# Sparse attention and a GELU layer on one core: the order of the first loads, and of two tables of work, is changed

## The chip, the core and the metric

The kernel runs on one core of a Trainium2 chip. A core has five engines, each with its own instruction stream: TensorE (PE in the profile, with its weight loads as PEld), VectorE (DVE), ScalarE (ACT), GpSimd (POOL) and SyncE (SP). They meet through semaphores. Transfers are asked for by POOL (software queue) or SP (hardware queue) and moved by 16 DMA engines that all of them share. The metric is the device time of one execution in microseconds (us); lower is better.

## The reference

Block-sparse attention over 4 batches, 8 heads, 768 positions, head size 64, in blocks of 32 (24 blocks). Its output, laid out by token, goes through a two-layer network with an exact GELU.

```python
scores = scale * np.matmul(q, k.transpose(0, 1, 3, 2))
mask = np.abs(blk_i - blk_j) <= window                      # window 1
mask = mask | (blk_i == 0) | (blk_j == 0) | (blk_i == n_blocks - 1) | (blk_j == n_blocks - 1)
for qb in range(n_blocks):
    for kb in sampled_blocks[qb]:                           # 3 drawn blocks
        mask[qb * block:(qb + 1) * block, kb * block:(kb + 1) * block] = True
scores = np.where(mask, scores, -1000000000.0)
attn = exp(scores - max) / (sum + 1e-09)
x = (attn @ v) laid out as [3072 tokens, 512]
h = x @ w_in                                                # 512 x 2048
out = (0.5 * h * (1.0 + erf(h / sqrt(2)))) @ w_out          # 2048 x 512
```

## The kernel before

The work is cut into eight units, two to a batch, of three blocks of 128 tokens each. A unit has an attention stage, then the first layer (`ffn1_step`, L551: w_in against the unit's `xT`, GELU into `g`); its second layer (`ffn2_pieces`, L576: `g` against w_out) is spread as filler over the attention stage of the next unit. The first unit of a batch also does the two dense rows of blocks (rounds 0 to 3); the other rounds take two query blocks each and form groups (`groups`; for the first unit group 0, 1 and 2).

What stands in which order is written out by hand. `attention` (L616) reads a string of words for each unit: `s` scores on PE, `m` maxima on DVE, `e` exponentials on ACT, `t` turning on DVE, `w` values on PE, `d` division on DVE, `o`/`O` outputs (PE, then ACT), `f3` three products of filler on PE, `S` the store of a finished block, `G` the load of the GELU table, `x...` a named extra step. The first unit's string stands at L731 and its filler is idle products that feed nothing (L589); the second's is `PLANS[1]` (L749), where `xk0` to `xk3` and `xq0` to `xq3` turn a pair of heads of the second batch's k or q on PE (L242) and place it by ACT, or by DVE with a `d` behind.

The first unit is fed by POOL, and POOL's order is the program's order of the calls from L181 on: k and q of batch 0, eight requests for V (`load_values`, one per head, L149), the numbers of the sampled blocks (`block_numbers`, L231, a load into the engine's registers, per group), then copies of the sampled key blocks (`gather`, L317, out of `k0`, which lies in the tile qT), then by `values_of` (L706) copies of the sampled value blocks out of `kv` into free places in `kn` (group 0) and `g` (groups 1, 2). Between these stand the requests for w_in in quarters (`load_w_in`, L162) and for w_out in halves (`load_w_out`, L167); behind the last copy, by `later_keys` (L719), those for k and q of batch 1, in halves of four heads.

SP carries six small transfers out of `k0` into `gb` early on (`fixed(t, nc.sync, 1)`, L303 to L307: the first and last key block for groups 1 and 2, 96 KB each), and all stores. The software requests take eight semaphores in turn, so each waits for the landing of the eighth before it.

Of the kernel before, what the change touches and what calls it, by code (L numbers as in the profile page):

```python
# [11 lines left out]
BF16 = mybir.dt.bfloat16  # L12
# [8 lines left out]
def kernel(  # L21
# [10 lines left out]
    nc = tc.nc  # L32
    P = 128
    B, H, S, D = q.shape
# [9 lines left out]
    VS = 2 * D + 4  # L44
    KC = NPR * BL
# [13 lines left out]
    const = ctx.enter_context(tc.tile_pool(name="const", bufs=1))  # L59
# [11 lines left out]
    kvs = [const.tile([P, NB + 1, BW], BF16, name=f"kv{i}") for i in range(2)]  # L71
# [10 lines left out]
    g = const.tile([P, KOUT, UT], BF16, name="g")  # L82
    mark = const.tile([1, 1], BF16, name="mark")
    junk = const.tile([1, 1], BF16, name="junk")

    HALVES = (slice(0, 4), slice(4, 8))

# [57 lines left out]
    def load_v(b, h):  # L145
        G, hh = divmod(h, 4)
        c0 = KC + VS * G + D * (hh % 2)
        hh ^= G
        nc.gpsimd.dma_start(out=kvs[b % 2][32 * hh:32 * hh + 32, 0:NB, c0:c0 + D],  # L149
                            in_=v[b, h].rearrange("(n p) d -> p n d", p=BL))  # L150


    VORDER = sorted(range(H), key=lambda h: (h // 4, (h % 4 ^ h // 4) % 2, h % 4))

    def load_values(b, at=slice(None)):
        for h in VORDER[at]:
            load_v(b, h)

    def load_w_in(part, n=4):
        w = D_FF // n  # L160
        cols = slice(w * part, w * part + w)
        nc.gpsimd.dma_start(  # L162
            out=w_in_sb[:, :, cols], in_=moe_w_in[:, cols].rearrange("(ki p) f -> p ki f", p=P))

    def load_w_out(part, n=4):
        w = KOUT // n
        nc.gpsimd.dma_start(  # L167
            out=w_out_sb[:, w * part:w * part + w, :],
            in_=moe_w_out[P * w * part:P * w * (part + 1)].rearrange("(ko p) f -> p ko f", p=P))
# [5 lines left out]
    def ones(i):  # L175
        for hh in range(4):
            for G in range(2):
# [6 lines left out]
                      in_=bass.AP(tensor=sb_words, offset=0,  # L184
                                  ap=[[NB * NR * 2, 1], [1, NB * NR * 2]]))
# [40 lines left out]
    def block_numbers(js, engine):  # L226
        flat = vf.rearrange("o j r -> o (j r)")
        vals = []
        for c0 in range(js[0] * NR, (js[-1] + 1) * NR, 22):
            c1 = min(c0 + 22, (js[-1] + 1) * NR)  # L230
            _, got = nc.values_load_multi_w_load_instructions(  # L231
                flat[0:1, c0:c1], engines=[engine], min_val=0, max_val=NB,
                skip_runtime_bounds_check_because="block numbers are below the number of blocks")
            vals += got if isinstance(got, (tuple, list)) else [got]
        return {j: vals[NR * i:NR * i + NR] for i, j in enumerate(js)}
# [46 lines left out]
    def gather_fixed(kT, place, copy=None, part=None, lanes=range(3)):  # L282

        copy = copy or nc.vector.tensor_copy
        groups = gb.rearrange("p (g x) -> p g x", x=GW)
        js = sorted(place)
        runs = [[j for j in js if place[j] - j == c] for c in sorted({place[j] - j for j in js})]
        for run in runs if part != 1 else ():
            i0 = place[run[0]]
            assert i0 % 3 == 0  # L290
            for lane in range(min(3, len(run))):
                if lane not in lanes:
                    continue
                m, g0 = len(range(lane, len(run), 3)), i0 // 3
                c0, j = BW + KC * lane, run[0] + lane - 1
                copy(
                    groups[:, g0:g0 + m, c0:c0 + 3 * BW].rearrange("p g (w c) -> p g w c", c=BW)[:, :, :, 0:KC],
                    kT[:, j:j + 3 * m, :].rearrange("p (g w) c -> p g w c", w=3))
        if part == 0:
            return  # L300
        at = slice(min(place.values()) // 3, max(place.values()) // 3 + 1)
        n = at.stop - at.start
        for to, n0 in ((groups[:, at, 0:3 * KC].rearrange("p g (l c) -> p g l c", c=KC), 0),  # L303
                       (groups[:, at, 4 * BW:GW].rearrange("p g (l x) -> p g l x", x=DW)[:, :, :, NR * BW:DW], NB - 1)):
            if copy is nc.sync:
                for x in range(n):
                    nc.sync.dma_start(out=to[:, x], in_=kT[:, n0:n0 + 1, :].to_broadcast([P, 3, KC]))  # L307
            else:
                copy(to, kT[:, None, n0:n0 + 1, :].to_broadcast([P, n, 3, KC]))

    def gather(unit, js, at, c0=0, c1=BW, engine=None):

        src = k0 if (unit.b, c1) == (0, KC) else kvs[unit.b % 2][:, :, c0:c1]
        for j in js:
            for r in range(NR):
                to = sampled_values(unit, j, r) if c0 == KC else sampled(unit.place[j], r)[:, c0:c1]
                (engine or nc.vector).tensor_copy(to[:, None, :], src[:, bass.ds(at[j][r], 1), :])  # L317
# [271 lines left out]
    def idle_products(m):  # L589

        op = psO.tile([P, D_MODEL], F32, name="op", tag="op")
        for _ in range(m):
            nc.tensor.matmul(op, lhsT=identity, rhs=qT0[:, 0:2, 0:2, :], start=True, stop=True)
            yield
# [77 lines left out]
    grps = units[0].groups  # L672
    value_list()
    others = block_numbers(grps[1], POOL)
    load_values(0, slice(3, 7))
    others |= block_numbers(grps[2], POOL)
    load_values(0, slice(7, None))
    known = block_numbers(grps[0], DVE)
    nc.vector.memset(kvs[1][:, FILLED:NB + 1, KC:BW], 0.0)
    known |= block_numbers(J0[7:9], DVE)  # L680
# [14 lines left out]
    def fixed(t, *how):  # L695
        gather_fixed(k0, {j: units[0].place[j] for j in grps[t]}, *how)
    fixed(1, nc.sync, 1)
    fixed(2, nc.sync, 1)
    gather(units[0], grps[1][:2], others, 0, KC, nc.gpsimd)
    load_w_in(0)  # L700
# [5 lines left out]
    def values_of(t):  # L706

        def ask():
            js = grps[t]
            gather(units[0], js[:3], others, KC, BW, nc.gpsimd)  # L710
            if t != 1:
                load_w_in(2 + t // 2)
            gather(units[0], js[3:], others, KC, BW, nc.gpsimd)
            if t == 2:
                load_w_out(0, 2)
                load_w_out(1, 2)
        return ask
# [7 lines left out]
    def more_numbers(js):  # L725
        def load():
            for c in range(0, len(js), 6):
                known.update(block_numbers(js[c:c + 6], DVE))
        return load
    attention(units[0], idle_products(32),  # L730
# [3 lines left out]
              {"l": later_keys, "p2": partial(later_pair, 0), "p3": partial(later_pair, 1),  # L734
               "h": lambda: fixed(0, None, 0, (0,)), "i": lambda: fixed(0, None, 0, (1, 2)),
               "j": lambda: fixed(0, None, 1),
# [7 lines left out]
    def next_keys(b):  # L744
# [1 line left out]
        spare_key(keys(b))  # L746

    PLANS = {
# [17 lines left out]
    for n, unit in enumerate(units):  # L766
# [3 lines left out]
        if nxt is not None and not fresh:  # L770
            if n == 0:
                nc.vector.tensor_copy(kvs[0][:, :, 0:KC], k0)
                more_numbers(J1[3:8])()
            gather_fixed(keys(b), nxt.place)
            gather(nxt, J1[:8], known)
            if n == 0:
                more_numbers(J0[:3])()
        for s in range(KOUT // 2):
            ffn1_step(n, 2 * s)
            if s == 0:  # L780
# [4 lines left out]
                elif fresh and b + 2 < B:  # L785
                    xT, t0 = column[b, unit.groups[-2][0]]
# [17 lines left out]
            if fresh and s == 0:  # L804
                gather_fixed(keys(b + 1), nxt.place)
                gather(nxt, J0[3:9], known)
                gather(nxt, J0[:3], known)
                hold_loads(sampled(nxt.place[J0[2]], NR - 1)[0:1, BW - 1:BW])
                gather(nxt, J0[9:], others, engine=nc.gpsimd)
# [43 lines left out]
```

## Time and profile before

| | |
|---|---|
| runs, median of 3 | 274.44 us (274.05 to 274.59) |
| profiled execution, device time | 273.89 us |
| its span, first to last instruction | 271.9 us |
| mean granted TensorE clock | 0.994 |
| busy: PE / DVE / ACT / POOL | 255.1 / 203.2 / 207.0 / 103.0 us |

The profile's times count from the span's first instruction. A row of the timeline gives start, length, engine, source line, operation, tiles written and read, count, and in brackets how long the engine had been idle and what ended that. A row of the stretches gives the busy time (and instruction count) of PE, PEld, DVE, ACT and POOL, the granted TensorE clock, the DMA engines' mean share and the GB/s moved. "issue" is a wait for nothing that the profile shows.

### The profile page before, as it was taken

What the parts mean: (1) busy time and instruction counts of PE and PEld (TensorE: products, weight loads), DVE (VectorE), ACT (ScalarE), POOL (GpSimd) and SP (SyncE); (2) the same over time, 40 slices, a digit from 0 to 9 for tenths busy, and PEclk for the clock granted to TensorE, in tenths of its full rate; (3) what the DMA queues carried; (4) which work ended last, traced back from release to release, by engine and by line L of the source; (5) the groups of instructions that cost most, each with busy time, mean ns of one, the idle gap of its engine ahead of it and who ended that gap; (6) DMA issues with size and microseconds to landing.
All of it is one profiled execution on the core that took longest, in us unless ns stands there. A gap on an engine that the chain in (4) does not pass through costs nothing.

```text
span 271.9 us, 11545 instructions
## 1 busy us (share of the span) xinstructions
PE 255.1 (94%) x4944; PEld 144.8 (53%) x4944; DVE 203.2 (75%) x472; ACT 207.0 (76%) x379; POOL 103.0 (38%) x212
## 2 busy tenths in 40 slices
PE   0789699999999999999999999999999999999995
PEld 0634485455664665545554466455645655465544
DVE  7599758699896989589998987698939993882000
ACT  8789746977868886797868976988788966995611
POOL 7798960735964000950963002920040160000000
PEclk9999979999999999999999999999999999999999
DMA  6999399979999115951999108911101110111012
GB/s 98 185 185 144 66 140 201 206 129 146 95 172 129 41 43 122 122 65 50 104 164 123 60 28 159 112 43 45 40 0 41 46 41 0 41 41 43 0 40 78
DMA packets 75909, 24.40 MB, mean 90 GB/s; under 512 B 65489, under 2 KB 72914, under 8 KB 75858
## 3 DMA queue, kind: packets, MB, share of 16 engines
q0 software_dynamic: 57440, 13.64, 53.7%
q1 hardware_dynamic: 18418, 10.03, 15.5%
q8 instruction: 38, 0.62, 1.0%
q14 instruction: 13, 0.11, 0.1%
HBM read 27.26 MB, written 6.29 MB: 123 GB/s over the span
## 4 chain that ended last, share of the span: by engine, by line
PE 71%; DMA 9%; ACT 7%; POOL 6%; issue 4%; DVE 2%; POOLq 1%; ACTq 0%
PE hp L540 27%; PE op L583 21%; PE av L484 9%; DMA kn<-in_k_dram 6%; PE sc L358 4%; DMA kv<-in_v_dram 3%; ACT L429 2%; PE tx L516 2%; PE op L612 2%; PE av L445 2%; POOL g L317 2%; ACT pp L401 2%; PE pt L242 1%; POOL kv L149 1%; PE av L612 1%
## 5 line engine op out<-in xcount | busy, mean ns | idle before, releaser
L540 PE MATMUL hp<-xT,w_in_sb 128*128 128x384 bf16 (+2 forms) x536 | 85.1, 319 | 0.2 <-issue 0.2
L583 PE MATMUL op<-w_out_sb,g 128*128 128x512 bf16 x336 | 83.9, 380 | 0.4 <-issue 0.4
L401 ACT ACTIVATE pp<-sc,nm 128x256 bf16<-128x256 f32 x176 | 74.4, 546 | 7.5 <-DVE nm L384 7.5
L540 PEld LDWEIGHTS <-w_in_sb 128*128 128x128 bf16 x536 | 51.2, 98 | 33.3 <-issue 0.3
L562 ACT ACTIVATE g<-hp 128x768 bf16<-128x768 f32 x56 | 45.2, 809 | 25.4 <-PE hp L540 25.4
L384 DVE TENSOR_REDUCE nm<-sc 128x4 f32<-128x1024 f32 (+1 forms) x48 | 53.2, 1117 | 10.5 <-PE sc L358 10.2
L583 PEld LDWEIGHTS <-g 128*128 128x128 bf16 x336 | 28.6, 98 | 34.3 <-issue 7.2
L317 DVE COPY gb<-kv 128x392 bf16 x177 | 34.7, 274 | 0.0
L418 DVE STREAM_TRANSPOSE pT<-pp 128x512 f32<-128x512 f32 (+1 forms) x48 | 31.2, 657 | 4.3 <-ACT pp L401 3.8
L317 POOL COPY gb<-kv 128x392 bf16 x54 | 26.3, 537 | 16.1 <-PE av L484 15.7
L173 POOL COPY mark<-gb 1x1 bf16<-1x1 bf16 x6 | 1.1, 178 | 81.3 <-DVE gb L317 81.3
L484 PE MATMUL av<-kv,pT 64*32 64x130 bf16 (+1 forms) x1344 | 28.7, 228 | 1.0 <-DVE pT L418 0.9
L484 PEld LDWEIGHTS <-pT 64*32 64x32 bf16 (+1 forms) x2400 | 26.8, 94 | 5.1 <-DVE pT L418 2.6
L149 POOL DMA_DIRECT2D kv<-in_v_dram x32 | 22.9, 726 | 2.4 <-issue 2.3
L524 ACT COPY xT<-tx 128x512 bf16<-128x512 bf16 (+1 forms) x32 | 13.9, 459 | 11.6 <-PE tx L516 11.3
L358 PE MATMUL sc<-gb,qT 64*32 64x256 bf16 x704 | 18.4, 274 | 2.9 <-issue 1.5
L358 PEld LDWEIGHTS <-qT 64*32 64x32 bf16 x832 | 9.5, 89 | 21.2 <-issue 13.4
L429 ACT ACT_TABLE_LOAD x15 | 19.2, 1283 | 0.2
L387 DVE TENSOR_REDUCE nm<-sc 128x1 f32<-128x768 f32 x16 | 14.7, 947 | 5.9 <-PE sc L358 5.7
L504 DVE TENSOR_TENSOR xh<-av,rec 128x512 bf16<-128x512 f32 (+2 forms) x28 | 18.3, 652 | 1.0
L567 ACT COPY os<-op 128x512 f32<-128x512 f32 (+1 forms) x23 | 13.1, 570 | 6.0 <-PE op L612 4.3
L484 PE MATMUL av<-gb,pT 64*32 64x130 bf16 x924 | 17.2, 222 | 0.0
(80 smaller groups left out, 249.6 us busy)
## 6 DMA issues: line engine op xcount, KB each, us to landing
out_dram<-os SPq DMA_DIRECT2D x23, 256.0 KB, 2.4
kv<-in_v_dram POOLq DMA_DIRECT2D x32, 96.0 KB, 3.7
w_in_sb<-in_moe_w_in_dram POOLq DMA_DIRECT2D x4, 512.0 KB, 7.3
w_out_sb<-in_moe_w_out_dram POOLq DMA_DIRECT2D x2, 1024.0 KB, 13.4
kn<-in_k_dram POOLq DMA_DIRECT2D x4, 384.0 KB, 11.4
qn<-in_q_dram POOLq DMA_DIRECT2D x4, 384.0 KB, 12.8
qn<-in_q_dram POOLq DMA_DIRECT2D x12, 128.0 KB, 4.9
kn<-in_k_dram POOLq DMA_DIRECT2D x12, 128.0 KB, 6.0
```

Source lines behind the costliest of these rows:

```text
L149: nc.gpsimd.dma_start(out=kvs[b % 2][32 * hh:32 * hh + 32, 0:NB, c0:c0 + D], in_=v[b, h].rearrange("(n p) d -> p n d", p=BL))
L317: (engine or nc.vector).tensor_copy(to[:, None, :], src[:, bass.ds(at[j][r], 1), :])
L358: nc.tensor.matmul(o, lhsT=qT[rows, j // 4, pr, BL * (j % 4):BL * (j % 4) + BL], rhs=rhs(rows, pr), start=True, stop=True)
L384: nc.vector.tensor_reduce(out=nm[:, 0:2 * n].rearrange("p (g j) -> p g j", g=2), in_=A4[:, :, 0:n, :], op=ALU.max, axis=AX.X, negate=True)
L401: nc.scalar.activation(at[:, x // n, x % n], A[:, a:a + 256].rearrange("p (e c k) -> p e c k", e=2, k=BL), AF.Exp, bias=nm[:, x:x + 1])
L418: nc.vector.transpose(pt.rearrange("p g c x -> p (g c) x")[:, :, 64 * s:64 * (s + n)].bitcast(F32), pp[:, 0:512 * n].bitcast(F32).rearrang ...
L429: nc.scalar.activation(junk, zero[0:1, 0:1], func)
L484: nc.tensor.matmul(av[32 * s:32 * (s + w), h, VS * G:VS * G + V2], lhsT=pv[rows, G, c % 4, BL * s:BL * (s + w), c // 4], rhs=src[rows], st ...
L504: nc.vector.tensor_tensor(xh[rows, :, 0:m * D].rearrange("p h (g x d) -> p h g x d", x=2, d=D), a[:, :, :, 0:2 * D].rearrange("p h g (x d) ...
L540: nc.tensor.matmul(hp[:, i, c0:c1], lhsT=w_in_sb[:, ki, (m + i) * P:(m + i + 1) * P], rhs=xTs[n % 2][:, ki, c0:c1], start=(ki == 0), stop= ...
L562: nc.scalar.activation(g[:, m:m + 2, 0:T], hp[:, :, 0:T], AF.Gelu)
L583: nc.tensor.matmul(op, lhsT=g[:, m, t * P:(t + 1) * P], rhs=w_out_sb[:, m, :], start=(m == 0), stop=(m == KOUT - 1))
```

## The change

It has four parts. POOL asks for the last V part ahead of loading group 2's numbers. SP gets a transfer of two values out of the last V part into a new tile `seen`, ahead of group 2's two key transfers: it waits for that part to land, and the two behind it with it. The third quarter of w_in, which stood among group 0's value copies, is asked for with the fourth, behind the last value copy. The strings of the first unit and of `PLANS[1]` are written anew. (`gather_fixed` names an expression; that changes nothing.)

```diff
+    seen = const.tile([1, 2], BF16, name="seen")
...
     others = block_numbers(grps[1], POOL)
-    load_values(0, slice(3, 7))
+    load_values(0, slice(3, None))
     others |= block_numbers(grps[2], POOL)
-    load_values(0, slice(7, None))
     known = block_numbers(grps[0], DVE)
...
     fixed(1, nc.sync, 1)
+
+    hh, c0 = VORDER[-1] % 4 ^ VORDER[-1] // 4, KC + VS * (VORDER[-1] // 4) + D * (VORDER[-1] % 2)
+    nc.sync.dma_start(out=seen, in_=kvs[0][32 * hh:32 * hh + 1, 0, c0:c0 + 2])
     fixed(2, nc.sync, 1)
...
             gather(units[0], js[:3], others, KC, BW, nc.gpsimd)
-            if t != 1:
-                load_w_in(2 + t // 2)
+            if t == 2:
+                load_w_in(2)
+                load_w_in(3)
             gather(units[0], js[3:], others, KC, BW, nc.gpsimd)
...
     PLANS = {
-        1: ("S s0 s1 m0 m1 f8 e0 f5 xk0d t0 f3 e1 s2 f3 xk1 m2 S t1 s3 e2 f3 m3 f2 xq1d xv t2 wa da e3  "
...
+        1: ("S s0 m0 s1 m1 e0 f10 e1 f3 t0 s2 xk1 t1 f3 m2 s3 f2 m3 xk0 f5 xq0d e2 f1 wa s4 e3 xk3 t2 da  "
...
```

Group 2 has three blocks, so `js[3:]` is empty there and both quarters stand behind the last value copy. On POOL, at the start, the V requests (`kv0`) and the loads of numbers (`vf`) stood like this, with what each waits for:

```order
L149 DMA kv0_86<-in_v_dram 32x24x64 x3
L231 TENSOR_LOAD vf_127 [waits DVE_49]
L149 DMA kv0_86<-in_v_dram 32x24x64
L149 DMA kv0_86<-in_v_dram 32x24x64 [waits DMASW0_49]
L149 DMA kv0_86<-in_v_dram 32x24x64 [waits DMASW1_49]
L149 DMA kv0_86<-in_v_dram 32x24x64 [waits DMASW2_49]
L231 TENSOR_LOAD vf_127
L149 DMA kv0_86<-in_v_dram 32x24x64 [waits DMASW3_49]
```

and now, at the same place:

```order
L150 DMA kv0_86<-in_v_dram 32x24x64 x3
L232 TENSOR_LOAD vf_128 [waits DVE_49]
L150 DMA kv0_86<-in_v_dram 32x24x64
L150 DMA kv0_86<-in_v_dram 32x24x64 [waits DMASW0_49]
L150 DMA kv0_86<-in_v_dram 32x24x64 [waits DMASW1_49]
L150 DMA kv0_86<-in_v_dram 32x24x64 [waits DMASW2_49]
L150 DMA kv0_86<-in_v_dram 32x24x64 [waits DMASW3_49]
L232 TENSOR_LOAD vf_128
```

The last request stands ahead of the second load of numbers. It still waits for DMASW3, the semaphore of q's second half. On POOL behind the value copies, where the weights and the next batch are asked for, the rows before were (the third quarter of w_in stands 49 rows ahead of the first of them, with group 0's copies):

```order
L162 DMA w_in_sb<-in_moe_w_in_dram 128x4x512
L167 DMA w_out_sb<-in_moe_w_out_dram 128x8x512 x2
L118 DMA kn<-in_k_dram 96x4x512
L118 DMA qn<-in_q_dram 96x4x512
L118 DMA kn<-in_k_dram 96x4x512
L118 DMA qn<-in_q_dram 96x4x512
```

and they now are:

```order
L163 DMA w_in_sb<-in_moe_w_in_dram 128x4x512 x2
L168 DMA w_out_sb<-in_moe_w_out_dram 128x8x512 x2
L119 DMA kn<-in_k_dram 96x4x512
L119 DMA qn<-in_q_dram 96x4x512
L119 DMA kn<-in_k_dram 96x4x512
L119 DMA qn<-in_q_dram 96x4x512
```

Two quarters of w_in now stand ahead of w_out and of the next batch's k and q. On PE, at the start of the second unit's attention stage, the first products of filler (`op`) and the first turn of the next batch's k (the weight load of `kn`) stood so, with the round of scores that comes next:

```order
L583 MATMUL op_1454<-w_out_sb_85,g_96 128x512 [waits DMASW0_49]
...
L583 MATMUL op_1454<-w_out_sb_85,g_96 128x512 [waits DMASW1_49]
...
L242 LDWEIGHTS kn_91 [waits DMASW2_49]
...
L583 LDWEIGHTS g_96 [waits Activation_49]
...
L358 LDWEIGHTS qT0_89 [waits DVE_49]
```

and now:

```order
L585 MATMUL op_1461<-w_out_sb_85,g_96 128x512 [waits DMASW0_49]
...
L585 MATMUL op_1461<-w_out_sb_85,g_96 128x512 [waits DMASW1_49]
...
L360 LDWEIGHTS qT0_89 [waits DVE_49]
L360 MATMUL sc_1482<-gb_88,qT0_89 32x256 [waits Activation_49]
...
L243 LDWEIGHTS kn_91 [waits DMASW2_49]
```

DMASW0 and DMASW1 are the two halves of w_out, read by the first and the ninth product; DMASW2 is the first half of k. The third round of scores has moved ahead of the first turn of k; the thirteen products and their two waits stand where they stood.

More of the change, by code (lines that the diff above doesn't have):

```diff
@@ L304, in gather_fixed @@
                        (groups[:, at, 4 * BW:GW].rearrange("p g (l x) -> p g l x", x=DW)[:, :, :, NR * BW:DW], NB - 1)):
+            fixed_block = kT[:, None, n0:n0 + 1, :].to_broadcast([P, n, 3, KC])
             if copy is nc.sync:
                 for x in range(n):
-                    nc.sync.dma_start(out=to[:, x], in_=kT[:, n0:n0 + 1, :].to_broadcast([P, 3, KC]))
+                    nc.sync.dma_start(out=to[:, x], in_=fixed_block[:, x])
             else:
-                copy(to, kT[:, None, n0:n0 + 1, :].to_broadcast([P, n, 3, KC]))
+                copy(to, fixed_block)
     def gather(unit, js, at, c0=0, c1=BW, engine=None):
```

10 rows, old and new, of tables (PLANS, js) are left out of this document.

## The prediction

> **What bounds the kernel now.** I read the page first, then the chain of work that ended last. TensorE (PE) is busy 94% of the span, so only PE's waits can be won. The chain over the first 76 us holds one long step that is not PE:
>
> ```profile
> PE 255.1 (94%) x4944; PEld 144.8 (53%) x4944; DVE 203.2 (75%) x472; ACT 207.0 (76%) x379; POOL 103.0 (38%) x212
> ```
> ```profile
> 33.55 0.69 POOL w_in_sb L162
> 34.24 1.73 POOL w_out_sb L167 x2
> 35.97 16.87 DMA kn<-in_k_dram
> 52.84 0.04 issue
> 52.88 0.53 PE pt L242 x16
> ...
> 66.92 0.44 issue
> ```
>
> GpSimd (POOL) asks for w_in's last quarter at 33.5, then for both halves of w_out, then for the second batch's k and q; PE's first turn of that k (the `pt` at 52.88) waits for it. Up to there the program runs at the pace of this row of transfers, which starts when POOL has made its last value copy. I then asked for POOL's timeline, the landings, and the stretches:
>
> ```profile
> 8.70 2.83 POOL L149 DMA_DIRECT2D kv<-in_v_dram  x4 [0.25 <-issue]
> 12.99 0.71 POOL L149 DMA_DIRECT2D kv<-in_v_dram  x1 [1.46 <-issue]
> 13.75 1.47 POOL L317 COPY gb<-qT 128x128 bf16 x6
> ...
> 18.24 2.17 POOL L317 COPY gb<-qT 128x128 bf16 x9
> 21.24 3.20 POOL L317 COPY kn<-kv 128x264 bf16 x9 [0.84 <-DMA kv<-in_v_dram]
> 24.39 0.74 POOL L162 DMA_DIRECT2D w_in_sb<-in_moe_w_in_dram  x1
> 25.12 1.10 POOL L317 COPY kn<-kv 128x264 bf16 x3
> 26.16 7.38 POOL L317 COPY g<-kv 128x264 bf16 x21
> 33.50 0.74 POOL L162 DMA_DIRECT2D w_in_sb<-in_moe_w_in_dram  x1
> 34.23 1.77 POOL L167 DMA_DIRECT2D w_out_sb<-in_moe_w_out_dram  x2
> ```
> ```profile
> DMA to landing us min/median/max: 10.9/13.4/15.9
> ```
> ```profile
> 30.00:32.00 2.00, 0.67 (x7) 0.31 (x6) 0.47 (x2) 0.91 (x3) 2.00 (x7) 1.00 0.00 0
> ...
> 34.00:36.00 2.00, 2.00 (x144) 2.00 (x132) 0.99 (x3) 0.00 (x0) 2.00 (x4) 0.50 0.47 22
> 36.00:38.00 2.00, 1.65 (x48) 1.28 (x31) 1.12 (x4) 0.58 (x1) 2.00 (x5) 0.81 1.19 196
> ...
> 50.00:52.00 2.00, 2.00 (x11) 0.88 (x9) 1.98 (x2) 1.99 (x5) 2.00 (x5) 1.00 1.24 206
> ```
>
> The last two figures of a stretch are DMA share and GB/s. The DMA is empty from 30 to about 35.5, then moves some 200 GB/s without a break. The landing row is that of w_out's two requests (34.23 and about 35.12): its second half lands 15.9 after 35.12, at 51.02. PE's own rows show how close that is:
>
> ```profile
> 27.08 0.41 PE L358 MATMUL sc<-gb,qT 64*32 64x256 bf16 x16 [0.35 <-ACT pp L401]
> ...
> 29.57 0.29 PE L358 MATMUL sc<-gb,qT 64*32 64x256 bf16 x4
> 31.33 0.29 PE L358 MATMUL sc<-gb,qT 64*32 64x256 bf16 x4 [1.47 <-issue]
> ...
> 49.44 2.98 PE L583 MATMUL op<-w_out_sb,g 128*128 128x512 bf16 x13
> 52.88 0.53 PE L242 MATMUL pt<-identity,kn 96*64 96x96 bf16 x16 [0.47 <-DMA kn<-in_k_dram]
> ```
> ```profile
> 258.10 3.45 PE op L612 x16
> ```
>
> Sixteen products of that size take 3.45 us, 0.216 each, so the ninth of those begun at 49.44, the first to read w_out's second half, stands at 51.17: 0.15 us after the landing. Then k's wait of 0.47. PE and the transfers are level here; whatever makes the transfers later is paid in full.
>
> **The change part by part.** *V ahead of the third group's numbers.* The last V request cannot leave before the second half of q has landed, since the software DMAs take eight semaphores in turn and it is the twelfth (the fourth was q's second half). PE saw that half at 12.02:
>
> ```profile
> 12.02 0.85 PE L242 MATMUL pt<-identity,qn 96*64 96x96 bf16 x16 [0.57 <-DMA qn<-in_q_dram]
> ```
>
> So it leaves at about 12.05 instead of 12.99. The numbers' load now stands behind it. Its 1.46 us either overlaps the request (copies from 13.5) or follows it (12.76 + 1.46 = 14.2), against 13.75 before: 0.25 earlier to 0.45 later. I take 0.2 later. The key copies then end at 20.41 + 0.2 = 20.6 (20.41 is the end of the row at 18.24). V's last part landed at 20.92:
>
> ```profile
> 12.99 7.93 DMA kv<-in_v_dram
> ```
>
> It gains at most the 0.94 of its earlier request, and is helped by the two of six key transfers (96 KB each, 0.2 MB, 1.0 us at 200 GB/s) that SyncE (SP) now holds until V is there: 20.0 to 20.9, so 20.3. The value copies begin at the later of both, 20.6 (20.2 to 20.9) instead of 21.24.
>
> *w_in's third quarter behind the copies.* The 33 value copies ran from 21.24 to 33.54 with one request between them, 24.44 to 25.12; without it they take 11.6 us. POOL comes to the weights at 32.2 (31.8 to 32.5), 1.3 earlier than 33.50. But the row of transfers now holds one quarter more: 0.524 MB at 206 GB/s, 2.55 us. Before, it was asked for at 24.39 and through when the DMA ran empty at 30; now it lies ahead of everything PE waits for. Net, w_out's second half and k land 2.55 - 1.3 = 1.25 later (0.85 to 1.55): 52.3 and 54.1. The quarter itself lands by 38, well before its use in the first layer, so for that move alone nothing waits.
>
> *The join on PE.* In the new order both score rounds, ten and three products and a third score round stand before the first turn of k (the order of rows is shown above). It starts at 54.1 instead of 52.88, with 0.34 us more of work done (the score round):
>
> ```profile
> 54.17 0.34 PE sc L358 x16
> ```
>
> That leaves +0.9 us. From there PE is nearly full:
>
> ```profile
> 53.42:72.19 18.77, 18.22 (x532) 10.31 (x533) 17.21 (x29) 14.68 (x29) 11.04 (x21) 1.00 1.19 125
> ```
>
> 18.22 of 18.77 busy: the new order can win at most 0.55. Against that stands one more of the eight turned pairs copied by ScalarE (five instead of four) behind two exponential rounds, and the next turn waits for its bank: some 0.3 by hand. I take -0.25 (-0.55 to +0.6). The sum so far is +0.65.
>
> *The first unit's new order.* The 1.47 us in the middle of a score round at 29.86 have no semaphore: instructions arriving late. The queue that carries instructions moved one packet just then, behind the tail of w_in's third quarter:
>
> ```profile
> q0 software_dynamic: 55, 0.04, 26.1%
> q8 instruction: 1, 0.02, 6.1%
> ```
>
> With that quarter gone this wait should go, and with it the slow clock that followed it:
>
> ```profile
> 29.94:33.35 3.41, 1.36 (x18) 0.74 (x17) 1.88 (x4) 1.86 (x6) 3.41 (x11) 1.00 0.02 5
> 33.35:36.76 3.41, 3.41 (x195) 3.19 (x192) 1.72 (x6) 0.48 (x2) 3.41 (x6) 0.50 0.53 55
> ```
> ```profile
> 33.03 3.29 PEld L484 LDWEIGHTS <-pT 64*128 64x128 bf16 x196 [0.82 <-DVE pT L418]
> ```
> ```profile
> 98.11 2.31 PE av L484 x193
> ```
>
> The same two value steps take 3.29 us at the granted clock of 0.50 and 2.31 in a later unit, so the first unit ends up to 1.47 + 0.98 = 2.5 us earlier (1.5 to 2.6). It earns nothing, because PE then comes earlier to a product whose weights come later: the wait at the ninth product becomes 51.17 - 2.5 = 48.7 to 52.3, some 3.6 us.
>
> *The clock in that wait.* The two stretches above show what a thinly used one costs: 1.36 busy of 3.41 at full clock, then 3.41 at 0.50. A wait of 2.5 to 3.7 us leaves a stretch as thin, unless it is split evenly between two. The price is the measured 0.98 (3.29 - 2.31); its ends are 0 and half of 3.41, 1.7. I take 1.0: the work behind the wait is as dense as those value steps. The Trainium skill, TensorE: Matmul & The Clock Gate, section on HAM oscillation, asks for no idle gap over some 3.4 us; by that rule a gap shorter than this keeps the clock and the sum stays without this term. This trace disagrees: its longest gap there was 1.47.
>
> Sum against the profiled execution: 273.89 (span 271.9) + 0.9 - 0.25 + 1.0 = 275.5. The median of the runs, 274.44, lies 0.55 above the profiled one, so **276.1**.
>
> **The rivals.** *(a) The transfers bind, the clock holds:* a split wait, or a shorter one because SP's two held key transfers land late:
>
> ```profile
> gb<-qT SPq DMA_DIRECT2D x6, 96.0 KB, 7.6
> ```
>
> They leave at about 21 and take a median of 7.6 us, so land at some 28.6; the first round that reads them ran at 27.08. This delay too is swallowed by the wait at w_out. 274.44 + 0.65 = 275.1.
>
> *(b) Faster:* the row of transfers absorbs the quarter. It decides if the quarter adds under 0.9 us rather than 2.55: k would land 0.4 earlier than before, the join would give -0.4 - 0.34 = -0.7 and the later order -0.25: 273.5. For it speaks the thin start (22 GB/s in 34 to 36); against it that a stretch in full flow moves 206 GB/s, where this would need 580.
>
> *(c) Still slower:* the second batch's V is asked for behind a pair that ScalarE now copies, about 63 instead of 59.03:
>
> ```profile
> 59.03 5.64 POOL L149 DMA_DIRECT2D kv<-in_v_dram  x8
> ```
>
> An instruction block then fetched through those requests may stall as at 29.86 (1.47) and not as at 66.92 (0.44): 1.0 more, 277.1. It decides if the fetch falls inside the eight requests.
>
> *(d) The pieces cancel:* POOL gets there at 31.8, the clock holds and the order wins all of its 0.55: 0.85 - 0.34 - 0.55, about nothing; 274.4.
>
> **How the numbers follow.** My forecast has 0.47, (a) 0.27, (b) 0.10, (c) 0.10, (d) 0.06. A measurement of this kernel can tell about 0.2%, 0.55 us, from no change. Faster by more than that is (b) and a little of (d): 0.11. Within it are most of (d) and a third of (a): 0.14. Slower: 0.75. The range runs from 274.0, (d) less the 0.4 by which the lowest of the runs (274.05) lies under their median, to 277.6, the forecast with the dear clock (0.7 more) and the late end of the new order (0.85 more); that leaves out (b) and the far part of (c).
>
> **What would show it.** Right: POOL's first value copy near 20.6 and the weights asked for near 32.2; the stall inside a score round near 30 gone; a DMA wait of 2.5 to 3.7 us in the first op products of the second unit, ended by w_out near 52.3; the first turn of k near 54.1; a granted clock of 0.5 for a stretch after it; from there equal work, and every later unit as before, only shifted. Wrong: w_out's second half landing by 51 or earlier (then (b)), or a first layer of unit one that waits for w_in.

## The result, and the profile after

The changed kernel is slower: 276.97 us against 274.25 us (medians of four runs each), a ratio of 1.0081 with a 95% interval of 1.0054 to 1.0107. Its profiled execution took 276.78 us with a span of 274.4, against 273.89 and 271.9 before, at a mean granted clock of 1.000 (0.994 before).

POOL's timeline of the changed kernel (start, length, engine, line, operation, tiles, count, and in brackets the idle time ahead) answers to the one shown in the prediction:

```profile
12.42 0.71 POOL L150 DMA_DIRECT2D kv<-in_v_dram  x1 [0.86 <-DMA qn<-in_q_dram]
16.38 1.48 POOL L319 COPY gb<-qT 128x128 bf16 x6 [3.25 <-DVE nm L389]
...
20.72 2.17 POOL L319 COPY gb<-qT 128x128 bf16 x9
22.85 4.26 POOL L319 COPY kn<-kv 128x264 bf16 x12
27.06 7.40 POOL L319 COPY g<-kv 128x264 bf16 x21
34.41 1.48 POOL L163 DMA_DIRECT2D w_in_sb<-in_moe_w_in_dram  x2
35.88 1.78 POOL L168 DMA_DIRECT2D w_out_sb<-in_moe_w_out_dram  x2
```

V's last request does leave earlier (12.42 instead of 12.99) and the value copies do run on without a break and without a wait for V. But POOL stands still for 3.25 us ahead of its first key copy, where it went straight on before (13.75). So the value copies begin at 22.85 instead of 21.24, and the weights are asked for at 34.41 instead of 33.50 (part of the lateness comes back there, since the third quarter's request no longer stands among the copies). What stands between the request and the copy is the load of group 2's numbers. That line's rows in the changed kernel and in the one before (count, shortest, median and longest in ns, first and last start) are:

```profile
L232 POOLq TENSOR_LOAD <-vf x1: 3689/3689/3689, 12.4 to 12.4; - x1
```
```profile
L231 POOLq TENSOR_LOAD <-vf x4: 827/1130/2273, 7.1 to 32.4; - x4
```

From 12.4, 3.69 us end at 16.1: that is POOL's gap. The longest one of the second row, 2273 ns, is the same load before the change. It started at 10.2, beside V requests that held POOL until 11.53 anyway. (The releaser in brackets, a maximum on VectorE, is inferred; run e7 shows below that it is not what POOL waited for.)

On the chain of work that ended last, and on PE's rows with a wait, the same lateness goes on:

```profile
37.62 18.05 DMA kn<-in_k_dram
```
```profile
32.08 1.04 PE L595 MATMUL op<-qT,identity 128*128 128x512 bf16 x4 [0.52 <-issue]
35.90 0.27 PE L486 MATMUL av<-kv,pT 64*32 64x130 bf16 x7 [1.15 <-issue]
...
41.82 7.80 PE L542 MATMUL hp<-xT,w_in_sb 128*128 128x384 bf16 x47 [0.82 <-issue]
53.85 1.24 PE L585 MATMUL op<-w_out_sb,g 128*128 128x512 bf16 x5 [1.84 <-DMA w_out_sb<-in_moe_w_out_dram]
55.72 0.53 PE L243 MATMUL pt<-identity,kn 96*64 96x96 bf16 x16 [0.29 <-DMA kn<-in_k_dram]
```

k was asked for at 35.97 and there at 52.84; now it is asked for at 37.62 and there at 55.67. Of these 2.83 us, 0.91 come from POOL's later arrival at the weights and the other 1.92 are put down to the quarter that now lies ahead of w_out; the same subtraction with k's first turn gives 2.00 in e2 and 1.92 in e5 below. PE's first turn of k starts 2.84 us later (55.72 instead of 52.88). The unit's first layer shows what is left of it (the row before, then after):

```profile
72.03 10.56 PE L540 MATMUL hp<-xT,w_in_sb 128*128 128x384 bf16 x64
```
```profile
74.35 10.56 PE L542 MATMUL hp<-xT,w_in_sb 128*128 128x384 bf16 x64
```

That is 2.32 us of the span's 2.5. The remaining units run equal but for 0.2, and 0.4 more lie outside of the span (276.78 - 274.4 against 273.89 - 271.9).

### The profile page after: what moved, and what is told of

It reads as the page before. It is cut to its first block, busy times and chain, and to the rows that moved or that the text cites. A ratio compares the mean times of both kernels' runs of the same rounds, so it can differ in the third digit from the quotient of the medians.

```text
span 274.4 us, 11553 instructions
## 1 busy us (share of the span) xinstructions
PE 255.1 (93%) x4944; PEld 142.9 (52%) x4944; DVE 203.6 (74%) x471; ACT 208.1 (76%) x380; POOL 103.8 (38%) x212
## 4 chain that ended last, share of the span: by engine, by line
PE 66%; POOL 8%; DMA 7%; ACT 7%; DVE 5%; issue 5%; POOLq 1%; ACTq 0%
PE hp L542 27%; PE op L585 19%; PE av L486 9%; DMA kn<-in_k_dram 7%; PE sc L360 4%; DVE nm L386 3%; ACT L431 2%; PE tx L518 2%; PE op L614 2%; POOL g L319 2%; ACT pp L403 2%; POOL kv L150 2%; DVE pT L420 1%; PE pt L243 1%; PE av L614 1%
## 5 line engine op out<-in xcount | busy, mean ns | idle before, releaser
L319 DVE COPY gb<-kv 128x392 bf16 x177 | 35.8, 281 | 0.0
L319 POOL COPY gb<-kv 128x392 bf16 x54 | 26.4, 539 | 16.1 <-PE av L486 15.7
L486 PE MATMUL av<-kv,pT 64*32 64x130 bf16 (+1 forms) x1344 | 27.7, 221 | 1.8 <-issue 1.5
L486 PEld LDWEIGHTS <-pT 64*32 64x32 bf16 (+1 forms) x2400 | 25.4, 91 | 6.3 <-issue 2.0
L526 ACT COPY xT<-tx 128x512 bf16<-128x512 bf16 (+1 forms) x32 | 13.9, 459 | 10.2 <-PE tx L518 10.1
L360 PEld LDWEIGHTS <-qT 64*32 64x32 bf16 x832 | 9.4, 90 | 20.8 <-issue 12.4
L407 ACT ACTIVATE pp<-sc,nm 128x768 bf16<-128x768 f32 x16 | 16.8, 1102 | 1.2 <-DVE nm L389 1.1
## 6 DMA issues: line engine op xcount, KB each, us to landing
qn<-in_q_dram POOLq DMA_DIRECT2D x4, 384.0 KB, 13.5
```

Source lines behind the costliest of these rows:

```text
L360: nc.tensor.matmul(o, lhsT=qT[rows, j // 4, pr, BL * (j % 4):BL * (j % 4) + BL], rhs=rhs(rows, pr), start=True, stop=True)
L486: nc.tensor.matmul(av[32 * s:32 * (s + w), h, VS * G:VS * G + V2], lhsT=pv[rows, G, c % 4, BL * s:BL * (s + w), c // 4], rhs=src[rows], st ...
```

## The experiments

Theory A in the texts on record is the reading just given: PE is held by the landing of w_out and k, which hangs on when POOL gets to ask for them and on what is queued ahead. The rivals are named in each text. Every run is compared with the kernel before on the same chip; e1 has 9 runs in the comparison, e6 has 6, the others 11 or 12, and an interval that includes 1 is taken as no change.

"Weights asked for" is the start of POOL's request for w_in's last quarter, or for the last two where they stand together.

| run | ratio to before (95%) | first key copy | weights asked for |
|---|---|---|---|
| the kernel before | 1 | 13.75 | 33.50 |
| the change | 1.0081 (1.0054 to 1.0107) | 16.38 | 34.41 |
| e1: V ahead alone | 1.0063 (1.0032 to 1.0093) | 17.05 | 35.75 |
| e2: quarter behind the copies alone | 1.0059 (1.0032 to 1.0086) | 13.87 | 32.53 |
| e3: new orders alone | 1.0005 (0.9976 to 1.0034) | 13.90 | 33.10 |
| e4: V marker on SP alone | 0.9990 (0.9964 to 1.0015) | 13.82 | 32.86 |
| e5: the change without V ahead | 1.0035 (1.0014 to 1.0056) | 14.08 | 32.32 |
| e6: the change without the moved quarter | 1.0136 (1.0097 to 1.0175) | 16.22 | 34.91 |
| e7: the change, numbers later | 1.0015 (0.9992 to 1.0038) | 13.51 | 32.37 |
| e8: V ahead, V marker, numbers later | 1.0028 (0.9999 to 1.0057) | 13.12 | 33.20 |
| e9: third quarter early, alone | 0.9979 (0.9948 to 1.0010) | 13.81 | 32.78 |
| e10: e7 with third quarter early | 1.0057 (1.0021 to 1.0092) | 13.11 | 32.74 |
| e11: e8 with third quarter early | 1.0048 (1.0017 to 1.0079) | 13.12 | 32.82 |
| e12: the change, numbers loaded twice | 1.0081 (1.0053 to 1.0109) | 16.55 | 34.62 |

### Each part alone

**e1**, the kernel before with V ahead of the numbers:

```diff
-    load_values(0, slice(3, 7))
+    load_values(0, slice(3, None))
     others |= block_numbers(grps[2], POOL)
-    load_values(0, slice(7, None))
```

> The kernel before with one part of the change: the last V part is asked for ahead of group 2's numbers. Theory A (the load of the numbers is exposed behind the last V request, and POOL reaches the weights later): POOL's first key copy near 16.4 instead of 13.75, the value copies from about 22.9 instead of 21.2, w_in's last quarter asked for near 35.2 instead of 33.5, k landing 1.4 to 1.7 later; the kernel 1.2 to 1.7 us slower. Theory B (the new orders cost the time, the requests are harmless): no change, within 0.4. Theory C (V lands earlier and that counts): 0.3 to 0.8 faster.

It cost 0.63% by itself. POOL's timeline and the numbers' load of this run show the same gap as in the change, a little longer:

```profile
12.71 0.71 POOL L149 DMA_DIRECT2D kv<-in_v_dram  x1 [1.19 <-DMA qn<-in_q_dram]
17.05 1.47 POOL L317 COPY gb<-qT 128x128 bf16 x6 [3.64 <-DVE gb L296]
```
```profile
L231 POOLq TENSOR_LOAD <-vf x1: 4071/4071/4071, 12.7 to 12.7; - x1
```

The late POOL is A's cause; the way to PE is not A's. k's first turn comes at 56.72 without a wait for it, so here PE was the late one. Its rows and the stretches of this run (busy time of PE, PEld, DVE, ACT, POOL; then granted clock, DMA share, GB/s) show where:

```profile
34.06 0.40 PE L358 MATMUL sc<-gb,qT 64*32 64x256 bf16 x4 [3.14 <-issue]
45.36 2.92 PE L540 MATMUL hp<-xT,w_in_sb 128*128 128x384 bf16 x17 [1.50 <-issue]
```
```profile
29.94:33.35 3.41, 0.98 (x8) 0.25 (x7) 0.90 (x2) 1.72 (x4) 3.41 (x11) 0.94 0.55 93
33.35:36.76 3.41, 2.68 (x50) 1.45 (x54) 2.23 (x4) 1.37 (x3) 3.41 (x10) 0.50 0.02 5
36.76:40.17 3.41, 3.41 (x189) 3.21 (x173) 1.46 (x6) 0.08 (x1) 3.41 (x5) 0.56 0.92 132
```

The third quarter, now asked for at 26.64, is still in flight at 30 (93 GB/s); the instruction wait inside the score round is 3.14 us instead of 1.47, and the clock then stands at 0.50 and 0.56 for two stretches instead of 0.50 for one. That the quarter in flight lengthened this wait is likely, but no run shows it by itself.

**e2**, the kernel before with only the third quarter behind the copies:

```diff
-            if t != 1:
-                load_w_in(2 + t // 2)
+            if t == 2:
+                load_w_in(2)
+                load_w_in(3)
```

> The kernel before with one part of the change: w_in's third quarter is asked for with the fourth. Theory A (the transfers ahead of w_out and k set the time): weights asked for near 32.8, 0.7 earlier, but a quarter more ahead of w_out; w_out's second half and k land 1.2 to 1.9 later; 1.0 to 1.9 us slower, with a wait for w_out at the ninth product. Theory B (the orders): no change, within 0.4. The stall of 1.47 in the score round near 30 should go either way, and the granted clock stay at 1.

It cost 0.59%, and PE's rows name the transfers:

```profile
52.12 1.24 PE L583 MATMUL op<-w_out_sb,g 128*128 128x512 bf16 x5 [1.59 <-DMA w_out_sb<-in_moe_w_out_dram]
53.91 0.53 PE L242 MATMUL pt<-identity,kn 96*64 96x96 bf16 x16 [0.56 <-DMA kn<-in_k_dram]
```

The instruction wait near 30 fell from 1.47 to 0.26 and PE reached the second unit earlier, where it waited. This is theory A, and it bears out that what the first unit wins is lost again at w_out. The profiled execution, 274.82 us, is the shortest of this run's twelve (median 276.36), so its rows show only a part of the loss.

**e3**, only the two new strings:

```diff
-              "xj xp2 xv0 s0 xp3 s1 m0 f1 xv1 f1 e0 xi m1 e1 xh s2 f1 s3 t0 xf0 m2 e2 f1 m3 t1 e3 f2 s4 xf1 f8 m4 "
...
+              "xf0 xj xh xp2 s0 xp3 m0 xv0 s1 f1 e0 xi s2 m1 e1 f1 s3 f1 t0 f1 m2 e2 m3 t1 e3 f3 s4 xv1 f1 m4 s5 "
...
```

> The kernel before with the two new order strings alone. Theory A: the row of transfers is unmoved (w_out's second half near 51, k near 52.9), PE starts the first turn of k when k lands with one score round more done; 0.2 to 0.7 us faster. Theory B (the orders cost the time): 0.5 to 2.5 us slower.

No change. Instruction waits of 0.27, 1.15 and 1.65 us stood in other places, the second unit's scores came at 50.87 instead of 48.87, and the transfers no longer held PE.

**e4**, only the V marker in SP's queue:

```diff
+    seen = const.tile([1, 2], BF16, name="seen")
...
     fixed(1, nc.sync, 1)
+    hh, c0 = VORDER[-1] % 4 ^ VORDER[-1] // 4, KC + VS * (VORDER[-1] // 4) + D * (VORDER[-1] % 2)
+    nc.sync.dma_start(out=seen, in_=kvs[0][32 * hh:32 * hh + 1, 0, c0:c0 + 2])
     fixed(2, nc.sync, 1)
```

> The kernel before with SP's transfer out of the last V part alone, so group 2's two key transfers wait for V. Theory A: V lands 0.5 to 0.9 earlier, POOL's value copies start near 20.4 instead of 21.24, the weights are asked for up to 0.8 earlier, k lands up to 0.8 earlier; 0 to 0.7 us faster unless PE is then late itself. Theory B: group 2's keys land near 28.5, its first score round (27.1 before) waits up to 1.4, and the first unit ends later; 0 to 1 us slower.

No change in time, although POOL's wait of 0.84 for V is gone and the weights are asked for 0.64 earlier (32.86). A small gain is not excluded: the spans of the eleven executions compared average 271.7 us, against 272.6 for the kernel before, while the device times, with what lies outside of the span, do not tell them apart.

### The change with one part taken out

**e5**, the change with V and the numbers in their old order:

```diff
-    load_values(0, slice(3, None))
+    load_values(0, slice(3, 7))
     others |= block_numbers(grps[2], POOL)
+    load_values(0, slice(7, None))
```

> The changed kernel with the V part's request back behind the load of group 2's numbers. Theory A (that load, exposed for some 3 us, makes POOL late): first key copy near 13.9 instead of 16.4, the weights asked for near 32.3 instead of 34.4, first turn of k near 53.8 instead of 55.7; 1.3 to 2.0 us faster than the changed kernel, so 0.5 to 1.2 slower than before. Theory B (the orders or the row of transfers alone cost it): within 0.4 of the changed kernel, 2 us slower than before.

Less than half of the loss stays: 0.35% instead of 0.81%. PE's waits:

```profile
41.17 7.80 PE L541 MATMUL hp<-xT,w_in_sb 128*128 128x384 bf16 x47 [1.10 <-issue]
51.75 1.24 PE L584 MATMUL op<-w_out_sb,g 128*128 128x512 bf16 x5 [0.39 <-DMA w_out_sb<-in_moe_w_out_dram]
53.62 0.53 PE L243 MATMUL pt<-identity,kn 96*64 96x96 bf16 x16 [0.29 <-DMA kn<-in_k_dram]
```

The first key copy is at 14.08, the weights are asked for at 32.32, and k's turn starts 2.1 us earlier than in the change. The span, 272.1, is 2.3 shorter than in the change. Theory A holds with its size, both for POOL and for the way to PE.

**e6**, the change with the third quarter in its old place:

```diff
-            if t == 2:
-                load_w_in(2)
-                load_w_in(3)
+            if t != 1:
+                load_w_in(2 + t // 2)
```

> The changed kernel with w_in's third quarter back among group 0's value copies. Theory A: POOL reaches the last quarter near 35.1, but without the other ahead of w_out; w_out's second half lands near 52.5 instead of 53.8, k near 54.3; 1 to 1.4 us faster than the changed kernel at best. Against it works what the V part alone showed: the third quarter asked for near 26.5 is in flight when PE's next instructions are fetched, and PE stalls 2 to 3 us near 30; then no faster than the changed kernel.

The slowest of all. The parts do not add: alone, the moved quarter cost 0.59%; with V ahead, leaving it where it was came out dearer than moving it (1.0136 against 1.0081, the intervals just overlap). As in e1, PE waits for no transfer but is late itself. The expected stall of 2 to 3 us did come, though not near 30 (0.70 there). Its wait ahead of the first layer is the longest of that kind there, and the same 47 products that take 7.80 us elsewhere take 9.48:

```profile
44.35 9.48 PE L541 MATMUL hp<-xT,w_in_sb 128*128 128x384 bf16 x47 [2.74 <-issue]
```
```profile
40.17:43.58 3.41, 1.44 (x21) 1.19 (x19) 1.54 (x4) 1.51 (x2) 0.00 (x0) 1.00 1.16 180
43.58:46.99 3.41, 2.63 (x12) 1.40 (x12) 3.34 (x14) 0.81 (x1) 0.00 (x0) 0.76 1.23 206
```

### The suspect moved

**e7**, the change with group 2's numbers loaded behind the first twelve key copies:

```diff
     load_values(0, slice(3, None))
-    others |= block_numbers(grps[2], POOL)
...
     load_w_in(1)
+    others |= block_numbers(grps[2], POOL)
     gather(units[0], grps[2], others, 0, KC, nc.gpsimd)
```

> The changed kernel with group 2's numbers loaded behind the first twelve key copies, where POOL's queue has copies in front. Theory A: first key copy near 13.2, the value copies near 20.5, the weights asked for near 32.2, first turn of k near 53.7; 1.5 to 2.2 us faster than the changed kernel, 0.3 to 1 us slower than before, since the third quarter still lies ahead of w_out. If the load is as dear there (2 to 3 us exposed), the gain is under 0.5.

POOL's timeline:

```profile
12.66 0.81 POOL L150 DMA_DIRECT2D kv<-in_v_dram  x1 [1.12 <-DMA qn<-in_q_dram]
13.51 1.47 POOL L318 COPY gb<-qT 128x128 bf16 x6
...
17.09 0.74 POOL L163 DMA_DIRECT2D w_in_sb<-in_moe_w_in_dram  x1
18.59 2.31 POOL L318 COPY gb<-qT 128x128 bf16 x9 [0.75 <-issue]
```

With V still ahead and only the load moved, the first key copy starts at 13.51 without a wait. So the 3.25 us were the load's; nothing else that the first copy needs was late. In its new place the load took 2.07 us, from 16.3 on, beside copies and a request, and only 0.75 of it shows. The time fell from 0.81% above the kernel before to 0.15%, with 1 inside the interval. This one line is worth most of the loss.

The trace does not show how PE gained by it. Its PE rows are:

```profile
37.47 0.27 PE L485 MATMUL av<-kv,pT 64*32 64x130 bf16 x7 [1.97 <-issue]
43.94 7.80 PE L541 MATMUL hp<-xT,w_in_sb 128*128 128x384 bf16 x47 [1.37 <-issue]
55.73 0.53 PE L243 MATMUL pt<-identity,kn 96*64 96x96 bf16 x16
```

k's first turn stands where it stood in the change (55.72), without a wait for a transfer: here PE itself was late, by instruction waits of 1.97 and 1.37 in place of 1.15 and 0.82. The profiled execution, 276.00 us, is one of the slowest of the twelve (median 275.12). So the times show what the load's place costs and this trace shows POOL's 2.04 us coming back; the way from there to PE is shown by e5.

**e8**, the kernel before with V ahead, the V marker, and the numbers as in e7 (orders and quarter as before):

> The kernel before with the V part first, group 2's numbers behind the first twelve key copies, and SP's transfer out of V; w_in and the orders as before. Theory A: value copies from about 20.4, the last quarter asked for near 32.7 (0.8 earlier), k landing near 52; 0.3 to 0.9 us faster than before, unless PE is held back by its instruction fetch (0.8 to 1.5 us near 30), then no change.

No gain: 1.0028 with 1 just inside the interval, although its profiled span, 270.7, is the shortest of all. Its twelve spans fall into two groups, seven from 270.7 to 272.1 and five from 273.8 to 274.3; the trace is of the first, so what made the second is not known.

### The quarter put elsewhere, and the load doubled

**e9**, the kernel before with the third quarter asked for directly behind the second:

```diff
     load_w_in(1)
+    load_w_in(2)
...
-            if t != 1:
-                load_w_in(2 + t // 2)
+            if t == 2:
+                load_w_in(3)
```

> The kernel before with one edit: w_in's third quarter is asked for directly behind the second, and no longer inside the first value copies. The order of the transfers in the queue stays as in the kernel before and POOL has the same requests, so the weights and k are asked for near 33.5 and k lands near 52.8. Theory A (k's landing binds the first unit in the kernel before, and PE's stalls lie under it): no change, 273.9 to 274.8 us. Rival B (PE's instruction stalls bind): the third quarter has landed by 30, the stall of 1.47 near 30 shrinks to under 0.6, and the time falls by 0.6 to 1.2 us. Rival C: the third quarter's packets now run beside the key copies' number loads, each of which grows towards 3 us, so POOL is 1 to 2 us later, and the time rises by as much.

**e10** is e7, and **e11** is e8, with this same edit:

> The change with two edits: group 2's numbers are loaded behind the first twelve key copies, as in the run e7, and w_in's third quarter is asked for directly behind the second. Against e7 (275.1 us) the quarter that lay between the value copies and w_out is gone from there. Theory A (in e7 PE itself was late, through its instruction stalls, and no transfer bound): 274.2 to 275.5, by how much of the stalls of 1.97 and 1.37 goes. If the transfers still bind in e7: 2 us lower, near 273.2. If the quarter beside the value copies makes the stalls grow: 275.5 to 277.

> The kernel before with V first, the wait for V's marker in SP's queue, group 2's numbers behind the first key copies (as in e8, 274.2 us), and w_in's third quarter directly behind the second. Everything that the runs so far found cheap, nothing they found dear. Theory A: k lands no later than in e8, the stall near 31 shrinks, 273.2 to 274.3 us. Rival: stalls of PE's instruction fetch take other places and the time stays 274.0 to 275.0.

e9 changed nothing, as theory A had it; e10 and e11 are slower than the kernel before, by 1.0057 and 1.0048, where e7 and e8 had 1.0015 and 1.0028. That they are slower than e7 and e8 is likely, but the intervals overlap. e10's 276.8 us lies in the highest of its three forecasts, and e11's 276.2 above both of its own. The instruction waits in the first unit did not grow in sum (0.54, 1.69 and 1.37 in e10 against 0.38, 1.97 and 1.37 in e7; 0.16 and 1.85 in e11 against 0.73, 0.28 and 1.02 in e8). In e11 another wait stands out. The transfers of SP's queue into `gb`, from 18 to 32 us, and the PE row that follows, first of e8 and then of e11:

```profile
gb<-qT SPq DMA_DIRECT2D x2, 96.0 KB, 4.4
```
```profile
27.48 0.41 PE L359 MATMUL sc<-gb,qT 64*32 64x256 bf16 x16 [0.42 <-ACT pp L402]
```
```profile
gb<-qT SPq DMA_DIRECT2D x2, 96.0 KB, 7.0
```
```profile
29.40 0.41 PE L359 MATMUL sc<-gb,qT 64*32 64x256 bf16 x16 [2.63 <-POOL g L318]
```

Beside the early quarter the two key transfers take 7.0 us instead of 4.4 to land. Asked for from 21.29, they are there by about 28.9, and the score round that reads them starts at 29.40. The bracket names a POOL copy, but in e8 the same copies began later (25.86, here 25.45) and nobody waited for them; the transfers are the likelier cause, by inference. A clock of 0.50 followed from 30.4 to 33.7. In e10 they also took 7.0 us, but there the delay does not carry on: the second unit's first layer starts at 74.12, against 74.13 in e7, and the 1.8 us by which its profiled span is longer come behind that, more than half of them in two instruction waits, 0.55 at 75.00 and 0.53 at 157.61. So what made e10 slower stays open.

**e12**, the change with the load of group 2's numbers written twice:

```diff
+    block_numbers(grps[2], POOL)
     others |= block_numbers(grps[2], POOL)
```

> The change, with the numbers of the third group loaded twice, one load directly behind the other, behind V's last request. It computes the same. Theory A (the load is exposed on POOL, and POOL's requests set k's landing): the second load takes 1 to 3.7 us more, the first key copy comes at 17.4 to 20, k lands as much later, and the time is 277.8 to 280.5 us. Rival (the 3.25 us before the first key copy are not the load's but a wait for VectorE's or ScalarE's work, or for a transfer that ends then anyway): the first key copy stays near 16.4 and the time at 276.5 to 277.4.

This did not become the experiment it was meant to be. The trace has four loads of numbers on POOL, as in the change; the one whose result nobody uses is not in the program:

```profile
L232 POOLq TENSOR_LOAD <-vf x4: 810/932/3822, 7.1 to 34.0; - x4
```

So it counts as a repeat of the change: 1.0081 again, the load 3.82 us and the gap ahead of the first key copy 3.46. It says nothing for the rival of its text.

No run is clearly faster than the kernel before. The lowest ratios, e9's and e4's, have 1 inside their intervals.

## Why the prediction came out as it did

| step | predicted | measured |
|---|---|---|
| V's last request | 12.05 | 12.42 |
| first key copy (by the sum's 0.2) | 13.95 | 16.38 |
| value copies begin | 20.6 | 22.85 |
| weights asked for | 32.2 | 34.41 |
| what the extra quarter adds to k's landing | 2.55 | 1.92 |
| PE's wait at w_out's second half | 2.5 to 3.7 | 1.84 |
| its end | 52.3 | 53.85 |
| k's first turn | 54.1 | 55.72 |
| join on PE | +0.9 | +2.5 |
| later order | -0.25 | -0.18 |
| slow clock behind the w_out wait | +1.0 | 0 |
| later units, and outside of the span | 0 | +0.6 |
| sum, profiled execution | 275.5 | 276.78 |

**The numbers' load: the step that failed.** The prediction said "Its 1.46 us either overlaps the request (copies from 13.5) or follows it". 1.46 was the idle time ahead of the old request, which holds the part of the load that showed, and not the load. The load's own row had 2273 ns, of which the V requests hid the rest. And moved to 12.4 it took 3.69 us. So overlapping did happen, and the copies still came at 16.38. The bounds 20.2 to 20.9 for the value copies had no room for that. From here POOL ran 2.2 us behind the forecast, and e7 shows that this was the load's doing.

**The quarter.** Its mechanism was right and e2 shows it alone: 1.59 at w_out and 0.56 at k. The size was too large by 0.63. The price came from a stretch in full flow, while the row of transfers starts thin (22 GB/s from 34 to 36 in the kernel before); that this makes the difference is likely, not shown.

**The join.** The forecast of +0.9 became 2.84 - 0.34 = +2.5, by POOL's 2.2 less the quarter's 0.6. With V and the numbers in their old order the same steps nearly fit: e5 asked for the weights at 32.32 (32.2), turned k at 53.62 (54.1), and took 274.97 us, where case (a) gave 275.1. In the change itself it was the first half of (a) that came, the transfers bind and the clock holds, at a far higher price; its second half did not, since no score round waited for the two held key transfers.

**The first unit.** The wait of 1.47 near 30 is gone, as said, and the slow clock with it: the stretches that stood at 1.36 busy and then 0.50 now read

```profile
29.94:33.35 3.41, 2.89 (x61) 1.29 (x46) 3.17 (x8) 3.15 (x9) 3.41 (x10) 1.00 0.02 5
33.35:36.76 3.41, 2.26 (x196) 1.91 (x196) 1.30 (x4) 2.07 (x3) 3.41 (x8) 1.00 0.26 13
```

But the unit did not end 2.5 us earlier. Waits of the same kind stand at 32.08, 35.90 and 41.82 (0.52 + 1.15 + 0.82 = 2.49), and the second unit's scores start at 49.55 instead of 48.87. So the wait at w_out was 1.84 and not some 3.6. "It earns nothing" held, for another reason than the one given.

**The clock behind that wait.** The +1.0 did not come: the clock stayed at 1.00. The rule of the Trainium skill (TensorE: Matmul & The Clock Gate, section on HAM oscillation) that the prediction set aside would have left this term out, and here its outcome agrees: a gap of 1.84, and no slow stretch. But waits of 2.63 (e11), 2.74 (e6) and 3.14 (e1), all shorter than that rule's gap, were each accompanied or followed by a clock of 0.50. So what failed in this term is the length of the wait; a wait of the forecast's 3.6 did not occur.

**The later order** won 0.18 of the 0.25 taken for it. The sum came near the measured time because a term of 1.0 that did not come stood in for 1.6 missing at the join. That the time fell inside the range is in this part luck. The direction and the path, transfers that land later and hold PE at w_out and k, were right. Of the listed signs the stall near 30 and the equal work behind did as forecast; the value copies, the requests for the weights, the wait's length and end, k's first turn and the slow clock did not.

## What to carry to other kernels

Before a load into an engine's registers is moved, read its own row for its length, and look for what of it is hidden in the old place; the idle time beside it shows only the rest. Moved behind the last request that covered it, it is paid nearly in full (3.25 of 3.69 us here), and it can itself grow. And when several engines and the transfers are level, taking out one wait by itself is worth little: e4 and e8 removed waits without a gain that is clear of the noise, while e1 and e2, which made POOL or the DMA queue later, were paid for.

## What the runs showed of the hardware that was not expected

**A load of the same nine numbers takes 2.1 to 4.1 us, by when it runs.** From 10.2 or 10.5: 2.27 (before) and 2.11 (e5). From 12.4 to 12.7: 3.69, 3.82, 4.07 and in e6 3.46. From 16.3: 2.07 (e7). The others on POOL took 0.8 to 1.3. The DMA share in the long one's time, in the changed kernel:

```profile
10.50:12.40 1.90, 1.28 (x34) 1.09 (x30) 1.73 (x13) 1.53 (x4) 1.06 (x2) 1.00 1.85 172
12.40:16.10 3.70, 3.47 (x49) 1.58 (x46) 3.41 (x8) 3.08 (x6) 0.71 (x1) 1.00 2.25 159
```

The slow ones fall where the DMA share is highest: 2.25 here and 2.15 in e1, against 1.82 for the 2.27 us before and 1.69 for the 2.07 us of e7. That they grow because of it is likely, but no run took those transfers away.

**PE's unexplained waits stand at fixed counts of instructions.** Between the waits at 32.08, 35.90, 41.82 and 61.67 in the changed kernel, PE and PEld ran these numbers of instructions (the counts behind the first two busy times):

```profile
32.08:35.90 3.82, 2.67 (x129) 1.84 (x129) 2.57 (x6) 3.09 (x6) 3.82 (x10) 1.00 0.08 6
35.90:41.82 5.92, 4.88 (x129) 4.04 (x129) 2.87 (x4) 2.46 (x5) 4.45 (x6) 1.00 1.17 179
41.82:61.67 19.85, 17.37 (x256) 9.16 (x256) 14.73 (x37) 14.30 (x28) 5.40 (x18) 1.00 1.17 200
```

That is 258, 258 and 512 in all, so steps of 256 but for the edges. The order of the work thus moves such a wait to other work but does not remove it. The Trainium skill (Runtime: NRT & Kernel Launch, section on instruction fetch mechanics) says that instructions come in blocks of 256 and that the cost of a block's edge is mostly hidden. The places agree with it. The cost does not always: it is 0.16 to 3.14 us here at the edges in the first unit that show a wait, though at the edge between 41.82 and 61.67 none is listed. The largest (e1) came with w_in's third quarter in flight, but e9 still had 0.95 with the DMA share at 0.02, so what sets the size stays open.

**The slow clock comes for 3.4 us at a time, and at a time of the run's own.** In steps of 0.1 us, the clock stood at 0.50 from 33.4 to 36.8 in the kernel before, from 33.0 to 39.8 in e1, from 45.4 to 48.8 in e6 and from 30.4 to 33.7 in e11: once or twice 3.4 us, so the stretches do not begin at the same point of every run. In the 3.41 us ahead of the fall PE was busy for 1.37, 1.37, 1.00 and 0.95 us. No slow stretch followed in the changed kernel, in e9 and in e7, where every 3.41 us from 20 to 90 us, wherever they are taken to begin, held at least 1.56, 1.56 and 1.44. In e2 the lowest is 1.28, around its wait for w_out, without a slow stretch; but a run without one does not show where its stretches begin, and others around the same wait hold up to 1.82. And in e1 a second slow stretch came although PE, at half clock, had been busy for 2.29. So a thin stretch stands ahead of each fall of the clock here, but what decides was not tried.
